# Long convolution and phase mixer: the set-up of the transform's tables rearranged

## Chip, cores and metric

The kernel runs on one core of a Trainium2 chip. The metric is the device time of one execution in microseconds, here the median of three runs. Engine names are those of the profile: PE (TensorE), PEld (its weight loads), DVE (VectorE), ACT (ScalarE), POOL (GpSimd) and SP (SyncE), which here only issues transfers.

## What is computed

```python
# x: (8, 5696, 128), h: (5696, 128)
L  = 2 * S                                   # 11392
Xf = rfft(x, n=L, axis=1); Hf = rfft(h, n=L, axis=0)
x  = irfft(Xf * Hf, n=L, axis=1)[:, :S, :]   # causal convolution, channel by channel
theta = x @ w_theta
y  = w_tok_r @ (x * cos(theta)) + w_tok_i @ (x * sin(theta))   # w_tok: 5696 x 5696
u  = x + y
out = u + relu(u @ w_ch)
```

## The kernel before

The convolution is a two-factor transform: 11392 = 178 x 64. The input is cut into 8 groups (two batches by half of the channels), and each group goes through four stages, all matmuls with DVE and ACT emptying PSUM:

- **First stage** (`stage_a`, L241): 16 chunks of four matmuls. The weights are columns of the input (`h16` or `x16`, 89 partitions by 128 columns picked with a stride), the moving operand is `f1_t`. ACT or DVE (`on_dve`) copies each chunk out.
- **Second stage** (`f2`, L260): 12 chunks, with the table `w_t2` as weights. For h, `h_chunk` (L323) scales the result into `hs` (ACT) and into `h_later` (DVE), which lies over `h16`. For x, `stage_b` (L391) copies to `xs` on ACT and multiplies with h's spectrum into `u_t` and `v_t` on DVE (L400).
- **Third stage** (`stage_c`, L410): 16 chunks with the inverse tables `r_u` and `r_v`, multiplied on the way out by the signs `sgn`, on DVE (L428) or ACT (L425, L426).
- **Fourth stage** (`stage_d`, L431): with the tables `e_t`.

h goes through the first two stages once, ahead of group 0. After that, group g's third stage is woven with group g+1's first, and its fourth with g+1's second (`woven` sorts closures by their place between 0 and 1). Then come the phases and the token mixing, which fill most of the time.

The set-up that matters here:

- h is loaded by two POOL transfers into `u_t` (L123), then copied on DVE into `h16` in two halves (L291). x's loads are 16 POOL transfers a group (`load_x`, L130) that convert to 16 bits on the way. `x16` has rows of `XP` = 68 columns, of which 64 are used; `h16` has rows of 64.
- `w_t2` has 90 slots of 192 columns. The upper and the lower 64 partitions hold the same slots shifted by 45. Sines for slots 0 to 44 are made in three blocks of 15 (`w_turns`, `w_angles`, `w_sines`). `w_rest(b)` (L203) completes a block: two scalings on DVE (L207, L208), and two copies on DVE (L210) of 64 partitions by 2880 that put each half's block into the other half's slots 45 and up. Every chunk of the second stage reads an original slot and a copied one: chunk 0 needs block 0, chunk 1 block 1 and chunk 3 block 2. `w_rest(0)` comes before h's copy, `w_rest(1)` after it, `w_rest(2)` after h's first stage.
- `h_other` (L330) and `h_store` (L335) are SP transfers: h's halves swapped within SBUF, and h stored to memory for later groups.
- `r_table(n)` (L344) makes one inverse table: index and turns on POOL (L155, L347, L351, L159), a subtraction on DVE (L162), a sine and two scalings on ACT (L168, L355, L356). `s_table` (L382) makes the signs in six small DVE instructions. Both tables and the signs are woven into group 0's second stage (L488).
- `e_index` and `e_table` make the seven steps of `e_t` likewise: POOL first, then DVE and ACT. Two steps that use the same scratch wait for one another.

Inside `in_order`, DVE, ACT and POOL keep the order of the program until L486; from there to the end of group 0's third stage DVE and ACT do, and POOL is ordered by the scheduler. `s_table` and `r_table` stood after that point, so their POOL part could be put between other POOL work:

```python
    in_order.close()
    in_order.enter_context(tc.manual_schedule(engines={mybir.EngineType.DVE, mybir.EngineType.Activation}))
    woven(b0, ([s_table, lambda: r_table(0, r_u), lambda: r_table(1, r_v)], 0.0, 0.6),
          [])
```

PSUM is used through `psum()`, four buffers of two banks, in all four stages.

Of the kernel before, what the change touches and what calls it, by code (L numbers as in the profile page):

```python
# [10 lines left out]
F32 = mybir.dt.float32  # L11
BF16 = mybir.dt.bfloat16
F16 = mybir.dt.float16
# [10 lines left out]
def kernel(  # L24
# [10 lines left out]
    nc = tc.nc  # L35
    B, S, D = x.shape
    assert D == 128
    P = 128
# [39 lines left out]
    N2 = 64  # L78
# [3 lines left out]
    KH = K1 // 2  # L82
    CK = 8
    HD = D // 2
    EN = N2 // 2 + 1
    WARM = 12
    XP = HD + 4
# [17 lines left out]
    def pool(name, bufs, stack, **kw):  # L105
        return stack.enter_context(tc.tile_pool(name=name, bufs=bufs, **kw))
# [9 lines left out]
    s1 = pool("set_1", 1, setup, side="right")  # L116
# [1 line left out]
    u_t = fc.tile([P, UVW + P], F16)  # L118
    v_t = fc.tile([P, UVW + P], F16)
    uv = [t[:, :UVW].rearrange("p (e d k) -> p e d k", e=2, k=K1) for t in (u_t, v_t)]  # L120
    h16 = s1.tile([P, 2, N2, HD], F16)
    for p0, p1 in ((0, 80), (80, NB)):
        nc.gpsimd.dma_start(u_t[p0:p1, :N2 * D],  # L123
                            bass.AP(tensor=h.tensor, offset=h.offset + p0 * N2 * D,
# [29 lines left out]
    def index(k, pattern, base):  # L154
        nc.gpsimd.iota(k, pattern=pattern, base=base, channel_multiplier=0,  # L155
                       allow_small_or_imprecise_dtypes=True)

    def up(t, k, eng=nc.vector):
        eng.tensor_scalar(k, t, MAGIC, None, op0=add)  # L159

    def below_one(t, k):
        nc.vector.scalar_tensor_tensor(t, k, MAGIC, t, op0=ALU.subtract, op1=ALU.subtract)  # L162
# [4 lines left out]
    def sine(out_, r, sign):  # L167
        nc.scalar.activation(out_, r, AF.Sin, bias=zero_b[:r.shape[0]], scale=-sign * TWO_PI)  # L168
# [4 lines left out]
    w_t2 = keep.tile([P, K1, 3 * N2], F16, tag="keep", name="w_t2")  # L173
# [3 lines left out]
    WS = 15  # L177
# [25 lines left out]
    def w_rest(b):  # L203
        s0 = WS * b
        here = w_t2[:, s0:s0 + WS]
        two = here[:, :, :2 * N2].rearrange("p k (f a n) -> p k f a n", f=2, a=2)
        nc.vector.tensor_scalar(two[:, :, :, 1], two[:, :, :, 0], odd, None, op0=mult)  # L207
        nc.vector.tensor_scalar(here[:, :, 2 * N2:], here[:, :, :N2], -1.0, None, op0=mult)  # L208
        for p0 in (0, 64):
            nc.vector.tensor_copy(w_t2[p0:p0 + 64, KH + s0:KH + s0 + WS],  # L210
                                  w_t2[64 - p0:P - p0, s0:s0 + WS])

    nc.scalar.activation(f1_t[:, :1], zero_b, AF.Sin, bias=zero_b)
    for b in range(len(w_of)):
# [22 lines left out]
    w_angles(2)  # L237
    w_sines(2)
    w_rest(0)

    def stage_a(lhs, on_dve=()):  # L241

        st = {}

        def chunk(q):
            if q == 0:
                st["a"] = fa.tile([P, 2 * K1, HD], F16, tag="a", name="a_")
            ps = psum()
            for i in range(4):
                nc.tensor.matmul(ps[:, i // 2, (i % 2) * 2 * K1:(i % 2 + 1) * 2 * K1], lhs(q + i), f1_t[:NB],  # L250
                                 start=True, stop=True)
            a_out = st["a"][:, :, q:q + 4].rearrange("p k (a q) -> p k a q", a=2)
            a_in = ps[:, :, :4 * K1].rearrange("p a (q k) -> p k a q", q=2)
            if q // 4 in on_dve:
                nc.vector.tensor_copy(a_out, a_in)
            else:
                nc.scalar.activation(a_out, a_in, AF.Copy)
        return [lambda q=q: chunk(q) for q in range(0, HD, 4)], st
# [19 lines left out]
    def woven(*lists):  # L278

        lists = [l if isinstance(l, tuple) else (l, 0.0, 1.0) for l in lists]  # L280
        steps = [(w0 + (i + 0.5) / len(l) * (w1 - w0), n, f)
                 for n, (l, w0, w1) in enumerate(lists) for i, f in enumerate(l)]
        for _, _, f in sorted(steps, key=lambda s: s[:2]):
            f()
# [7 lines left out]
                              u_t[:NB, :N2 * D].rearrange("p (n h d) -> p h n d", h=2, d=HD)[:, :, :, d0:d0 + 32])  # L292
    steps, a_h = stage_a(lambda q: h16[:NB].rearrange("p h n d -> p (h n) d")[:, :, q], (4, 6, 8, 10, 12, 14))
    w_rest(1)
    for f in steps:
        f()
    w_rest(2)

    nc.gpsimd.memset(u_t[:, UVW:], 0.0)
    nc.gpsimd.memset(v_t[:, UVW:], 0.0)  # L300
# [15 lines left out]
    def h_part(c):  # L316
        return h_flat(c).rearrange("p (r d k) -> p r d k", r=2, k=CHK[c][1])
# [5 lines left out]
    def h_chunk(c):  # L323
        c0, ck = CHK[c]
        ps = f2(a_h, c, False)
        nc.scalar.activation(h_part(c)[:, 0], ps[:, 0], AF.Copy, scale=16.0 / NF)
        nc.vector.tensor_scalar(h_later[:, HD * c0:HD * (c0 + ck)].rearrange("p (d k) -> p d k", k=ck),
                                ps[:, 1], 16.0 / NF, None, op0=mult)
# [10 lines left out]
    r_u = fc.tile([P, P], F16)  # L339
    r_v = fc.tile([P, P], F16)  # L340
    e_t = fc.tile([P, EN, 2, NB], F16)
    sgn = fc.tile([P, N2], F32)

    def r_table(n_, r_):  # L344
        t, k = (s1.tile([P, 2 * N2], F32, name=f"r_{n_}{q}") for q in "tk")
        index(k, [[0, 2], [1, N2]], 0)
        nc.gpsimd.tensor_scalar(t, k, lane[:, 0:1], 1.0 / N2, op0=mult, op1=mult)  # L347
        for q0 in range(2):
            for q1 in range(2):
                a_ = t[64 * q0:64 * q0 + 64, 64 * q1:64 * q1 + 64]  # L350
                nc.gpsimd.tensor_scalar(a_, a_, 0.25 * (1 + (1 - n_ if q0 else n_) + q0 - q1), None, op0=add)  # L351
        up(t, k, nc.gpsimd)
        below_one(t, k)
        sine(k, t, 1)
        nc.scalar.activation(r_[:, :N2 + EN], k[:, :N2 + EN], AF.Copy, scale=0.125)  # L355
        nc.scalar.activation(r_[:, N2 + EN:], k[:, N2 + EN:], AF.Copy, scale=-0.125)  # L356
# [5 lines left out]
    E_STEPS = [(n, n0, min(ES, EN - n0)) for n, n0 in enumerate(range(0, EN, ES))]  # L362
# [5 lines left out]
    def e_index(n, n0, cn):  # L368
        t, k = e_pair(n, cn)
        index(k, [[1, cn], [N2, NB]], n0)  # L370
        nc.gpsimd.tensor_scalar(t, k, lane[:K1, 1:2], 1.0 / NF, op0=mult, op1=mult)
        up(t, k, nc.gpsimd)
# [9 lines left out]
    def s_table():  # L382
        half, end = lane[:, 5:6], lane[:, 6:7]
        nc.vector.tensor_scalar(half, lane[:, 1:2], 0.0, -0.5, op0=ALU.is_equal, op1=mult)
        nc.vector.tensor_scalar(end, lane[:, 1:2], float(K1 - 1), -0.5, op0=ALU.is_equal, op1=mult)
        nc.vector.scalar_tensor_tensor(half, half, 1.0, end, op0=add, op1=add)
        nc.vector.memset(sgn, 1.0)
        nc.vector.tensor_scalar(sgn[:, :EN], sgn[:, :EN], half, None, op0=mult)
        nc.vector.tensor_scalar(sgn[:, EN:], sgn[:, EN:], odd, half, op0=mult, op1=mult)
# [76 lines left out]

    a0, b0 = front(0, (2, 4, 6, 8, 10, 12, 14))
    BATCH = ((0, 4), (4, 4), (8, 3), (11, 1))
    for c in range(NCK):
        h_chunk(c)  # L470
        for c0, n in HS:
            if c == c0 + n - 1:
                h_other(c0, n)
    for c0, n in BATCH:
        h_store(c0, n)
    for e_ in E_STEPS[:4]:
        e_index(*e_)
    for t, dst, mul in ((w_in[0], w_theta_sb, 1.0 / (2.0 * math.pi)), (w_in[1], w_ch_sb, 1.0)):
        nc.gpsimd.tensor_scalar(dst, t, mul, None, op0=mult)
    for n, f in enumerate(a0):  # L480
        f()
        if n == 9:
            e_table(*E_STEPS[0])
    load_x(1)
    e_index(*E_STEPS[4])
    in_order.close()  # L486
    in_order.enter_context(tc.manual_schedule(engines={mybir.EngineType.DVE, mybir.EngineType.Activation}))
    woven(b0, ([s_table, lambda: r_table(0, r_u), lambda: r_table(1, r_v)], 0.0, 0.6),  # L488
          [])
    e_left = [lambda f=f, n=n: f(*E_STEPS[n]) for f, n in (  # L490
        (e_table, 1), (e_index, 5), (e_table, 2), (e_index, 6), (e_table, 3),
        (e_table, 4), (e_table, 5), (e_table, 6))]
# [222 lines left out]
    for g, (bp, dh) in enumerate(groups):  # L715
        st = {}
        last = g + 1 == len(groups)
        if last:
            late_order.enter_context(tc.manual_schedule(engines={mybir.EngineType.Pool}))
        a_, b_ = front(g + 1, () if g else (5, 11))  # L720
        if last:
            for _ in range(3):
                steps0.pop(0)()
        now = [with_load(steps0.pop(0), n < 6) for n in range(9)] if last else []
        c_ = stage_c(st, last)
        if g + 2 < len(groups):
            a_ = a_ + [lambda g=g: load_x(g + 2)]
        woven((c_, 0.06 if a_ else 0.0, 1.0), (a_, 0.0, 0.55), now, ([] if g else e_left, 0.0, 0.9))
        if g == 0:
            in_order.close()  # L730
            first.close()
        if g + 2 == len(groups):
            xin.close()
            open_phases()
            load_ya0()
        now = [steps0.pop(0) for _ in range(5)] if last else []
        woven(b_, (stage_d(st, bp, dh, load_ya1 if last else None), 0.0, 1.1 if b_ else 1.0), now)
        if g + 2 == len(groups):
            load_ya1()
            open_ring()  # L740
# [320 lines left out]
    for i, (k, p, tt, j0, s0, nj) in enumerate(stretches):  # L1061
# [13 lines left out]
        if (p, tt, j0 + s0) == (0, 1, 0):  # L1075
            with tc.issue_after(sides["late"].ins):
# [4 lines left out]
        woven = (tt is not None and end_of_pair and i + 1 < len(stretches)  # L1081
                 and stretches[i + 1][2] is not None)
# [37 lines left out]
        if tt is None:  # L1120
            if p:
                aside(True, False)
            if first_of_pair:
                q = M1 if p else M3
# [16 lines left out]
            if end_of_pair:  # L1141
# [5 lines left out]
                c, c0 = c_last  # L1147
# [165 lines left out]
```

## Time and profile before

| | |
|---|---|
| median of three runs | 2041.6 us (2041.51 to 2042.7) |
| the profiled execution | 2038.09 us |
| its span | 2036.3 us |
| mean granted TensorE clock | 0.987 |
| PE busy | 1948.2 us, 96% of the span |
| DVE / POOL / ACT busy | 1574.1 / 974.3 / 654.7 us |

The span runs from the first to the last instruction of the profiled execution; 1.8 us lie around it. A row of a timeline gives the start, the busy time, the engine, the line, the operation, what it writes and reads, the count, and in brackets the idle time before it with what ended it. A row of a window gives its length, then the busy time of each engine with the count, the granted clock of PE, the share of the DMA engines (it can exceed 1, as transfers in flight are counted) and what they moved. A DMA issue is shown with its size and the time from issue to landing. Line numbers are those of the kernel before.

### The profile page before, as it was taken

What the parts mean: (1) busy time and instruction counts of PE and PEld (TensorE: products, weight loads), DVE (VectorE), ACT (ScalarE), POOL (GpSimd) and SP (SyncE); (2) the same over time, 40 slices, a digit from 0 to 9 for tenths busy, and PEclk for the clock granted to TensorE, in tenths of its full rate; (3) what the DMA queues carried; (4) which work ended last, traced back from release to release, by engine and by line L of the source; (5) the groups of instructions that cost most, each with busy time, mean ns of one, the idle gap of its engine ahead of it and who ended that gap; (6) DMA issues with size and microseconds to landing.
All of it is one profiled execution on the core that took longest, in us unless ns stands there. A gap on an engine that the chain in (4) does not pass through costs nothing.

```text
span 2036.3 us, 41470 instructions
## 1 busy us (share of the span) xinstructions
PE 1948.2 (96%) x15841; PEld 1074.5 (53%) x15841; DVE 1574.1 (77%) x2890; ACT 654.7 (32%) x1004; POOL 974.3 (48%) x1744
## 2 busy tenths in 40 slices
PE   5799999799999999999999998999999999999998
PEld 5688888654444444444444444444444444444444
DVE  8777778777788888888867668768677786777767
ACT  6788888862233323333300000111111111111111
POOL 8523321485353545454566454453544545354450
PEclk9899999899999999999999999999999999999999
DMA  9878975999798989999999799796977979788793
GB/s 117 62 84 124 88 83 167 255 268 186 161 174 179 174 171 167 181 167 181 165 176 154 117 251 220 127 154 125 154 134 138 155 128 154 129 153 140 133 156 85
DMA packets 491239, 312.56 MB, mean 153 GB/s; under 512 B 182983, under 2 KB 456007, under 8 KB 490055
## 3 DMA queue, kind: packets, MB, share of 16 engines
q0 software_dynamic: 322608, 158.13, 61.0%
q1 hardware_dynamic: 162448, 140.25, 24.1%
q10 hardware_dynamic: 5984, 11.54, 1.6%
q8 instruction: 124, 2.03, 0.4%
q14 instruction: 75, 0.61, 0.1%
HBM read 354.89 MB, written 90.82 MB: 219 GB/s over the span
## 4 chain that ended last, share of the span: by engine, by line
PE 67%; DVE 3%; DMA 3%; issue 1%; POOL 0%; ACT 0%; DVEq 0%; SPq 0%
PE m L1250 62%; DMA ring<-in_moe_w_tok_i_dram 2%; DVE c L1257 1%; PE utp L918 1%; PE v L925 1%; PE m L1254 1%; PE m L1137 1%; DVE b L776 1%; DVE wt L838 1%; PE tpz L866 0%; PE theta_ps L514 0%; POOL ring L627 0%; DMA wl<-in_moe_w_tok_i_dram 0%; DMA z_hbm<-mag 0%; DVE c L927 0%
## 5 line engine op out<-in xcount | busy, mean ns | idle before, releaser
L627 POOL DMA_DIRECT2D ring<-in_moe_w_tok_i_dram x720 | 388.2, 548 | 662.2 <-DVE wt L838 582.5
L627 POOL DMA_DIRECT2D ring<-in_moe_w_tok_r_dram x720 | 386.9, 549 | 122.6 <-DVE wt L838 64.2
L838 DVE STREAM_TRANSPOSE wt<-ring 128x384 f32<-128x384 f32 (+2 forms) x720 | 358.8, 523 | 103.2 <-PE m L1250 66.5
L1250 PE MATMUL m<-b,wt 128*128 128x512 bf16 x1640 | 388.4, 379 | 2.0 <-DVE wt L838 1.7
L1250 PEld LDWEIGHTS <-wt 128*128 128x128 bf16 x1804 | 176.0, 98 | 215.5 <-DVE wt L838 4.0
L1257 DVE TENSOR_TENSOR c<-c,m 128x512 f32<-128x512 f32 x412 | 265.3, 670 | 0.4 <-PE m L1250 0.4
L920 ACT ACTIVATE ring<-utp 128x512 bf16<-128x512 bf16 x85 | 50.8, 597 | 580.2 <-PE utp L918 580.2
L137 POOL DMA_DIRECT2D x<-in_x_dram x128 | 99.4, 798 | 141.5 <-PE ps L250 132.7
L420 PE MATMUL ps<-r_u,u_t 128*128 128x128 f16 x1024 | 125.2, 221 | 5.9 <-DVE u_t L400 2.9
L421 PE MATMUL ps<-r_v,v_t 128*128 128x128 f16 x1024 | 124.2, 220 | 0.3
L1167 PE MATMUL m<-b,wt 128*128 128x512 bf16 x480 | 112.8, 385 | 6.3 <-DMA b<-zz 2.8
L915 ACT ACTIVATE ub<-c 128x512 bf16<-128x512 f32 x88 | 55.1, 628 | 196.5 <-DMA ring<-in_moe_w_tok_i_dram 114.6
L421 PEld LDWEIGHTS <-v_t 128*128 128x128 f16 x1024 | 100.9, 99 | 5.2 <-issue 3.7
L420 PEld LDWEIGHTS <-u_t 128*128 128x128 f16 x1024 | 100.9, 99 | 3.9 <-DVE u_t L400 3.9
L398 ACT ACTIVATE xs<-ps 128x1024 f16<-128x1024 f32 x96 | 91.6, 983 | 9.6 <-PE ps L274 2.9
L400 DVE TENSOR_TENSOR u_t<-xs,hs 128x1024 f16<-128x1024 f16 x96 | 64.3, 670 | 32.1 <-ACT xs L398 29.9
L1167 PEld LDWEIGHTS <-wt 128*128 128x128 bf16 x528 | 51.1, 99 | 67.9 <-issue 4.8
L516 ACT ACTIVATE red<-theta_ps,magic 128x512 f32<-128x512 f32 (+1 forms) x46 | 31.6, 687 | 136.5 <-PE theta_ps L514 113.6
L268 PEld LDWEIGHTS <-w_t 64*128 64x128 f16 x3240 | 58.6, 100 | 23.6 <-issue 17.9
L868 ACT ACTIVATE ring<-tpz 128x512 bf16<-128x512 bf16 (+1 forms) x46 | 27.5, 597 | 130.8 <-PE tpz L866 113.7
L927 DVE SCALAR_TENSOR_TENSOR c<-v,c 128x512 f32<-128x512 f32 x88 | 59.9, 682 | 7.1 <-PE v L925 6.9
L400 DVE TENSOR_TENSOR v_t<-xs,hs 128x1024 f16<-128x1024 f16 x96 | 63.7, 664 | 0.0
(2934 smaller groups left out, 3816.1 us busy)
## 6 DMA issues: line engine op xcount, KB each, us to landing
ring<-in_moe_w_tok_r_dram POOLq DMA_DIRECT2D x352, 96.0 KB, 4.4
ring<-in_moe_w_tok_i_dram POOLq DMA_DIRECT2D x352, 96.0 KB, 4.7
ring<-in_moe_w_tok_r_dram POOLq DMA_DIRECT2D x352, 80.0 KB, 4.4
ring<-in_moe_w_tok_i_dram POOLq DMA_DIRECT2D x352, 80.0 KB, 3.9
cp_hbm<-c SPq DMA_DIRECT2D x88, 256.0 KB, 2.4
c<-cp_hbm SPq DMA_DIRECT2D x88, 256.0 KB, 4.5
out_dram<-c SPq DMA_DIRECT2D x88, 256.0 KB, 4.4
yy<-y_hbm SPq DMA_DIRECT2D x84, 128.0 KB, 2.4
```

Source lines behind the costliest of these rows:

```text
L137: nc.gpsimd.dma_start(x16[p0:p1, e, n0:n0 + 16, :HD], bass.AP(tensor=src.tensor, offset=src.offset + (p0 * N2 + n0) * D + dh * HD, ap=[[N2 ...
L268: nc.tensor.matmul(ps[:, e, j * HD:(j + 1) * HD], w_t2[rows, slot(e, c0 + j), N2 * (1 - ri):N2 * (3 - ri)], a_st["a"][rows, ri * K1 + c0 + ...
L398: nc.scalar.activation(xs[:, :, :, :ck], ps, AF.Copy)
L400: nc.vector.tensor_tensor(uv[r][:, :, :, c0:c0 + ck], xs[:, :, :, :ck], hv[:, r:r + 1].to_broadcast([P, 2, HD, ck]), op=mult)
L420: nc.tensor.matmul(o, u_t[:, at:at + P], r_u, start=True, stop=False)
L421: nc.tensor.matmul(o, v_t[:, at:at + P], r_v, start=False, stop=True)
L627: nc.gpsimd.dma_start(wb[32 * i:32 * i + 32, :ng, :nj * 64], bass.AP(tensor=a.tensor, offset=a.offset + row0 * S + p * H + i * QR + j0 * 6 ...
L838: nc.vector.transpose(wt.rearrange("p j t r -> p (j t r)").bitcast(F32).rearrange("p (j g t) -> p g j t", j=TJ, g=4)[:, :ng, :nj], wb[:, : ...
L927: nc.vector.scalar_tensor_tensor(c[:m], v[:m], 0.0, c[:m], op0=ALU.max, op1=ALU.add)
L1167: nc.tensor.matmul(ms[n // 2 * 2 + h], a[n][:, j, :, r], bts_of[p][jj][n % 2 * 2 + h][:, r, :], start=(n % 2 == 0 and jj == 0 and r == 0), ...
L1250: nc.tensor.matmul(ms[q], a[q][:, j, :, r], bts[jj][q][:, r, :], start=(jj == 0 and r == 0), stop=(jj == NJ - 1 and r == 1 and q not in left))
L1257: nc.vector.tensor_tensor(c, z, ms[q], op=op)
```

## The change

The second half of `w_t2` is filled by six SP transfers instead of six DVE copies, and `w_rest(2)` stands before h's first stage. `h16` gets rows of 68 columns. The signs and the first inverse table are made during h's second stage, the second one during group 0's first stage; their POOL part (`r_index`) stands ahead of h's second stage together with the first step of `e_index`, while three other steps of `e_index` stand after the load of group 1. Group 0's second stage is left with its own chunks alone. In group 0's third stage, group 1's first stage takes the places 0.2 to 0.75 instead of 0 to 0.55.

```diff
-    h16 = s1.tile([P, 2, N2, HD], F16)
+    h16 = s1.tile([P, 2, N2, XP], F16)
...
         for p0 in (0, 64):
-            nc.vector.tensor_copy(w_t2[p0:p0 + 64, KH + s0:KH + s0 + WS],
-                                  w_t2[64 - p0:P - p0, s0:s0 + WS])
+            nc.sync.dma_start(w_t2[p0:p0 + 64, KH + s0:KH + s0 + WS],
+                              w_t2[64 - p0:P - p0, s0:s0 + WS])
...
     w_rest(1)
+    w_rest(2)
     for f in steps:
         f()
-    w_rest(2)
...
-    def r_table(n_, r_):
-        t, k = (s1.tile([P, 2 * N2], F32, name=f"r_{n_}{q}") for q in "tk")
+    r_in = {}
+
+    def r_index(n_):
+        t, k = r_in[n_] = [s1.tile([P, 2 * N2], F32, name=f"r_{n_}{q}") for q in "tk"]
         index(k, [[0, 2], [1, N2]], 0)
...
         up(t, k, nc.gpsimd)
+
+    def r_table(n_, r_):
+        t, k = r_in[n_]
         below_one(t, k)
         sine(k, t, 1)
...
+    r_index(0)
+    r_index(1)
+    e_index(*E_STEPS[0])
     for c in range(NCK):
         h_chunk(c)
+        if c == 4:
+            s_table()
+        elif c == 9:
+            r_table(0, r_u)
...
-    for e_ in E_STEPS[:4]:
-        e_index(*e_)
+    e_index(*E_STEPS[1])
...
     for n, f in enumerate(a0):
         f()
+        if n == 2:
+            r_table(1, r_v)
         if n == 9:
             e_table(*E_STEPS[0])
     load_x(1)
-    e_index(*E_STEPS[4])
+    for e_ in E_STEPS[2:5]:
+        e_index(*e_)
...
-    woven(b0, ([s_table, lambda: r_table(0, r_u), lambda: r_table(1, r_v)], 0.0, 0.6),
-          [])
+    for f in b0:
+        f()
...
-        woven((c_, 0.06 if a_ else 0.0, 1.0), (a_, 0.0, 0.55), now, ([] if g else e_left, 0.0, 0.9))
+        woven((c_, 0.06 if a_ else 0.0, 1.0), (a_, 0.0 if g else 0.2, 0.55 if g else 0.75), now, ([] if g else e_left, 0.0, 0.9))
```

## Prediction

> **What bounds the kernel now.** I read the page first, then the windows of the set-up cut at its hand-overs, then the timeline, the tiles and the DMA issues in them. From the page:
>
> ```profile
> span 2036.3 us, 41470 instructions
> PE 1948.2 (96%) x15841; PEld 1074.5 (53%) x15841; DVE 1574.1 (77%) x2890; ACT 654.7 (32%) x1004; POOL 974.3 (48%) x1744
> ```
>
> PE is busy nearly all the time, so only an edit that lets PE begin or go on sooner can pay. The chain of waits, followed back from the end, breaks off near 530 us and does not reach the set-up. I therefore take the stages one by one. They hand over through a full wait each, and what follows (the other groups' transforms, the token mixing) is released by the stage ahead of it and not by a clock, so I carry a shift of the set-up to the end unchanged. Windows cut at PE's first instruction of each stage (columns: length, then busy time and count of PE, PEld, DVE, ACT and POOL, PE's granted clock, DMA share, GB/s):
>
> ```profile
> 0.00:16.05 16.05, 0.00 (x0) 0.01 (x1) 11.89 (x30) 7.59 (x13) 12.86 (x25) 1.00 1.75 133
> 16.05:26.75 10.70, 9.85 (x64) 9.61 (x65) 10.03 (x13) 7.38 (x10) 10.43 (x16) 1.00 1.41 85
> 26.75:35.42 8.67, 7.83 (x360) 7.44 (x360) 8.37 (x13) 6.00 (x11) 8.18 (x13) 1.00 0.34 73
> 35.42:44.30 8.88, 6.41 (x64) 5.58 (x64) 8.05 (x12) 8.01 (x13) 7.55 (x13) 1.00 0.43 95
> 44.30:66.03 21.73, 11.08 (x372) 9.94 (x371) 15.92 (x32) 13.82 (x20) 15.55 (x19) 0.66 1.32 142
> 66.03:91.95 25.92, 22.75 (x349) 22.03 (x349) 21.31 (x27) 19.96 (x33) 14.25 (x19) 0.89 0.55 35
> ```
>
> In order: tables and h's copy; h's first stage; h's second stage; group 0's first stage (x); its second stage with the products; its third stage with group 1's first. PE idles for 16 us, then is the bound in h's first stage, and is half idle in the 21.73 us of the products. DVE's timeline shows who holds the start:
>
> ```profile
> 12.40 2.06 DVE L210 COPY w_t<-w_t 64x2880 f16<-64x2880 f16 x2
> 14.49 2.68 DVE L291 COPY h<-u_t 89x4096 f16<-89x4096 f16 x2
> ...
> 27.39 2.16 DVE L210 COPY w_t<-w_t 64x2880 f16<-64x2880 f16 x2
> ...
> 29.59 4.88 DVE L327 TENSOR_SCALAR h<-ps 128x512 f16<-128x512 f32 x8
> ```
>
> h's copy begins the moment the w copies end, and PE begins at 16.05 with its first half. The third pair of w copies keeps DVE from h's second stage until 29.59. The tiles h and x, same instruction:
>
> ```profile
> L250 PEld LDWEIGHTS <-h x64: 168/174/210, 16.0 to 25.4; 89*128 89x128 f16 x64
> L250 PEld LDWEIGHTS <-x x64: 143/147/155, 35.0 to 43.1; 89*128 89x128 f16 x64
> ```
>
> Same shape, same granted clock (1.00); x has padded columns and loads faster. And in the products' stage:
>
> ```profile
> 52.48 0.40 ACT L168 ACTIVATE r_0k<-r_0t,zero_b 128x128 f32<-128x128 f32 x1 [1.56 <-DVE r_0t L162]
> ...
> 54.26 0.69 DVE L400 TENSOR_TENSOR u_t<-xs,hs 128x1024 f16<-128x1024 f16 x1 [1.81 <-ACT xs L398]
> ...
> 58.78 0.69 DVE L400 TENSOR_TENSOR u_t<-xs,hs 128x1024 f16<-128x1024 f16 x1 [1.81 <-ACT xs L398]
> ```
>
> Each inverse table makes ACT wait for DVE and then DVE for ACT.
>
> **The sum, part by part** (times from the span's start; negative is gained).
>
> *1. w copies off DVE.* DVE is free for h's copy at 12.40 instead of 14.49. h itself is later: its second transfer is issued at 2.31 and takes 10.3, so it lands at 12.6. Start 12.7 instead of 14.49: **-1.8**; PE then starts at 14.25.
>
> *2. Padded columns.* x's first stage has the same 64 matmuls and took 8.88 where h's took 10.70: **-1.8**. DVE keeps up: from 14.0 the copy's second half 1.38, w_rest(1)'s two scalings 1.24, w_rest(2)'s 1.17, six casts of 0.90, sum 9.2, ending at 23.2. That padding slows the copy itself isn't shown; its runs stay 32 columns, I take nothing. h's second stage starts at 23.15 (-3.6).
>
> *3. h's second stage* keeps its 8.67, which is PE's pace (0.72 a chunk). Added on DVE: the signs' six instructions 0.9 (47.63 to 48.5) and one subtraction 0.28, beside 7.0 of scalings (L327): 8.2. On ACT a sine and two scalings, 0.9, beside 6.4 (L326). Both stay below 8.67, so they hide in it; if that cover were gone they would cost 1.2. New is that chunks wait for the w transfers. Each of the six moves 64 x 5760 B = 360 KB. The nearest rows:
>
> ```profile
> hs<-hs SPq DMA_DIRECT2D x14, 64.0 KB, 2.7
> hs<-hs SPq DMA_DIRECT2D x2, 256.0 KB, 3.7
> hf_hbm<-h SPq DMA_DIRECT2D x1, 384.0 KB, 8.0
> ```
>
> (KB each, us from issue to landing.) So 4 to 8 us each; one issue takes SP 0.6 (L333). The first pair leaves at 12.5 and lands by 20 (due 23.2); the second leaves at 16.7, lands at 21 to 25 (due at chunk 1, 23.9); the third leaves at 18, lands at 22 to 26.6 (due at chunk 3, 25.3). A wait of 0 to 1.3: I take **+0.7**. On SP nothing is queued behind them before h's halves at 27, which the products need 15 us later.
>
> *4. POOL's queue.* r_index(0), r_index(1) and e_index(0) now stand in order behind x's load, and r_table(0) makes DVE, and ACT behind it, wait for the first. x's load shares the engines with 2.2 MB of w. The nearest row is group 1's load beside the 1.44 MB of hf stores: POOL needed 15.6 for it (43.74 to 59.34), 12.3 for the next one with nothing beside it (82.01), so 3.3 more; by bytes 4.9 here. POOL then is free of loads at 23.6 + 4.9 = 28.5. r_index is 2.9 of POOL time undisturbed (as for r_1), 4.0 disturbed (as for r_0), so it is ready at 31.4 to 32.5, against chunk 9 at 31. A wait of 0.4 to 1.5, of which the psum buffers cover some: **+0.5**. x itself landed near 25 (DMA share 0.00 from 25 to 26) and lands at 30: hidden. x's first stage starts at 33.0 instead of 35.42.
>
> *5. r_table(1) in x's first stage*: ACT 0.9, DVE 0.28, where ACT is busy 8.01 of 8.88: **+0.7**. The products start at 42.6 (was 44.30).
>
> *6. Products' stage without tables.* DVE has 11 chunks at a pitch of 1.21 and a short one of 0.7, 14.0; 2.1 before the first and 0.2 after the last: 16.3. e_index(2) to (4) now run on POOL after group 1's load, that is inside this stage; the one that did so before stretched two products by 0.35 each, so +0.7: 17.0 instead of 21.73, **-4.7**. The third stage starts at 59.6 instead of 66.03.
>
> *7. Third stage, group 1's first stage moved from 0-0.55 to 0.2-0.75.* ACT has less to do early and more late. In the second half ACT would have 6 evacuations of 0.7, 4 sign scalings of 1.15 and 4 tables of 1.15, 13.8; DVE has 12 in the first half: 25.8, as now. If the clock of PE is still at half at the start, up to 2.6 more; if the late tables overlap, or the clock is full (DVE waited 0.95 and 1.68 there on PE at half clock), up to 2.5 less. I take **+0.7**. load_x(1) starts about 2 us sooner, so x lands before its new place.
>
> Sum: -1.8 -1.8 +0.7 +0.5 +0.7 -4.7 +0.7 = **-5.7**. The profiled execution took 2038.09 (span 2036.3 and 1.8 around it), 3.5 below the median of 2041.6; its counterpart would be 2032.4, and from the median I forecast **2035.9**.
>
> [...]
>
> **Rivals.**
> *Better*: w lands in time, POOL in time, and the products without gaps keep the clock at 1.00: steps 3 and 4 give 0 and step 7 -2.0. Sum -9.6, 2032.0. For it: 310 to 368 GB/s were reached from 47 to 50. Against: the loads beside. 0.15.
> *Half rate*: 2.2 MB at 192 GB/s (the hs rows: 192 KB more take 1.0 longer), 11.5 us, all of it taken from x's load. POOL is free at 35.1, r_index(0) ready at 38, x's first stage in effect starts at 38.5. Net, with steps 5 to 7, is that start minus 38.7: -0.2, 2041.4. 0.11.
> *Padding does nothing* (h's slower loads come from something else): step 2 falls out, -3.9, 2037.7. 0.08.
> *Slower: POOL's queue becomes the bound.* Place: DVE at chunk 9, waiting for r_index(0). With d the delay of x's load and disturbed index work (4.0), the start is 23.6 + d + 4.0 + 0.5, and r_table(1) waits 2.0 more for its own index, due 1.5 later. It breaks even at d = 8.6 and is slower by 0.2% from d = 12.7; were the six transfers served with half overlap (6 x 3.7 = 22 at none), d is near 15 and the time 2048. For it: POOL did wait on x's own transfers (3.7 in all). Against: the 3.3 us beside 1.44 MB. 0.11.
>
> **How the numbers follow.** About 0.2%, 4.1 us, is what a measurement of this kernel can tell from no change. The forecast has 0.55; its centre is 1.6 beyond that bound, so I put 0.47 of it as faster and 0.08 within. Faster 0.47 + 0.15 = 0.62; within 0.08 + 0.11 + 0.08 = 0.27; slower 0.11. The range takes in the better rival and reaches up to the half rate: 2031 to 2042; left out are the slower rival and some of the two ends.
>
> **What would show it.** L250 on h at x's 147 ns and PE's first matmul near 14.3; no DVE wait ahead of the first h scaling; DVE idle ahead of r_0's subtraction below 1.5; L400 unbroken at a pitch of 0.60; the third stage starting near 59.6. Wrong if PE waits for w transfers in h's second stage for over 2 us, if x's load ends on POOL after 32, or if the third stage grows by over 3.

## The result, and the profile after

The change makes the kernel slower: 2045.54 us against 2040.73 (medians of 13 runs each), ratio 1.003 [1.0018, 1.0042]. The forecast was 2035.9 with a range of 2031 to 2042. The profiled execution took 2048.25, against 2038.09 before. Of these 10 us the set-up accounts for 5.1, close to the difference of the medians, 4.8; the rest lies in the two thousand microseconds behind it and isn't traced here (the 13 times of the kernel after alone spread from 2042.94 to 2053.06). From the page:

```profile
span 2046.5 us, 41302 instructions
PE 1940.1 (95%) x15664; PEld 1075.9 (53%) x15841; DVE 1568.9 (77%) x2884; ACT 654.3 (32%) x1004; POOL 970.1 (47%) x1744
```

The windows, cut at the same hand-overs as before (length, then busy time and count of PE, PEld, DVE, ACT and POOL, PE's granted clock, DMA share, GB/s):

```profile
0.00:14.03 14.03, 0.00 (x0) 0.00 (x1) 9.54 (x28) 7.59 (x13) 10.84 (x23) 1.00 1.51 132
14.03:24.71 10.68, 9.82 (x65) 9.59 (x65) 8.85 (x11) 7.38 (x10) 6.91 (x9) 1.00 1.90 152
24.71:41.24 16.53, 10.00 (x360) 9.26 (x360) 7.12 (x16) 5.86 (x10) 8.73 (x21) 0.92 1.50 170
41.24:53.35 12.11, 9.99 (x68) 9.54 (x65) 8.73 (x14) 9.63 (x19) 4.51 (x7) 0.50 0.51 164
53.35:69.72 16.37, 8.67 (x361) 8.12 (x360) 14.03 (x24) 11.48 (x12) 12.22 (x17) 0.71 1.46 92
69.72:98.14 28.42, 22.96 (x361) 21.89 (x362) 22.20 (x27) 21.04 (x35) 18.52 (x24) 0.95 0.33 22
```

Against before the lengths went by -2.0 (start), 0.0 (h's first stage), +7.9 (h's second), +3.2 (x's first), -5.4 (products), +2.5 (third stage): +6.2 where group 1's second stage begins, and +5.1 at its third stage. One border isn't the same in both kernels: before, 12 matmuls of group 1's first stage ran ahead of 66.03 (372 matmuls in the products' row and 349 in the next), and after, none did (361 and 361). Some work thus moved from the products to the third stage, and -5.4 and +2.5 are best read together, as -2.9.

PE's timeline of the long third row, in the kernel before:

```profile
26.75 6.59 PE L268 MATMUL ps<-a__184,w_t 64*128 64x64 f16 x287 [0.86 <-ACT a__184 L257]
33.83 1.24 PE L268 MATMUL ps<-a__184,w_t 64*128 64x64 f16 x73 [0.48 <-issue]
35.42 5.92 PE L250 MATMUL ps<-f_t,x 89*128 89x180 f16 x56 [0.36 <-DVE h L327]
```

And in the kernel after:

```profile
24.71 1.81 PE L268 MATMUL ps<-a__188,w_t 64*128 64x64 f16 x61 [0.86 <-ACT a__188 L257]
28.23 1.90 PE L268 MATMUL ps<-a__188,w_t 64*128 64x64 f16 x62 [1.71 <-DMA w_t<-w_t]
30.78 0.24 PE L268 MATMUL ps<-a__188,w_t 64*128 64x64 f16 x2 [0.64 <-DVE h L327]
31.53 1.14 PE L268 MATMUL ps<-a__188,w_t 64*128 64x64 f16 x34 [0.52 <-DMA w_t<-w_t]
33.26 2.86 PE L268 MATMUL ps<-a__188,w_t 64*128 64x64 f16 x128 [0.59 <-issue]
39.18 2.13 PE L268 MATMUL ps<-a__188,w_t 64*128 64x64 f16 x73 [3.06 <-issue]
```

The idle times, 1.71 + 0.64 + 0.52 + 0.59 + 3.06 = 6.5, and 10.0 of work (7.83 before) make the 16.5. PE waits twice for copies of w that are still in flight, and for 3.06 us for nothing that the profile names. The transfers of x in the kernel before (KB each, median us from issue to landing) and POOL's first issue behind x's load:

```profile
x<-in_x_dram POOLq DMA_DIRECT2D x8, 160.0 KB, 5.5
```

```profile
22.15 0.59 POOL L289 DMA_DIRECT2D w_in<-in_moe_w_theta_dram  x1
```

The same in the kernel after, with the transfers of w:

```profile
w_t<-w_t SPq DMA_DIRECT2D x6, 360.0 KB, 10.8
x<-in_x_dram POOLq DMA_DIRECT2D x8, 160.0 KB, 12.8
```

```profile
31.53 0.59 POOL L289 DMA_DIRECT2D w_in<-in_moe_w_theta_dram  x1 [7.25 <-DMA x<-in_x_dram]
```

I had taken 4 to 8 us for a w transfer: they took 7.8 to 12.6. Six of them leave from 12.42 to 19.63, and the last lands at 31.5. x's load, which runs beside them, suffers as much: its 160 KB pieces needed 5.5 us before and 12.8 now (those issued after 14 us: 4.1 to 4.9 before, 16.9 to 17.8 now), and POOL came to the issue behind them 9.4 us later. And the tile x, first before and then after:

```profile
L250 PE MATMUL ps<-f_t,x x64: 237/241/241, 35.4 to 43.2; 89*128 89x180 f16 x64
```

```profile
L250 PEld LDWEIGHTS <-x x64: 147/168/173, 41.2 to 52.0; 89*128 89x128 f16 x64
L250 PE MATMUL ps<-f_t,x x64: 310/356/373, 41.2 to 52.1; 89*128 89x180 f16 x64
```

After the gaps PE's granted clock is 0.50, and x with its padded columns shows the very figures that h showed without padding.

### The profile page after: what moved, and what is told of

Same layout as the page of the kernel before. It is cut to its first block, busy times and chain, and to the rows that moved or that the text cites. A ratio compares the mean times of both kernels' runs of the same rounds, so it can differ in the third digit from the quotient of the medians.

```text
span 2046.5 us, 41302 instructions
## 1 busy us (share of the span) xinstructions
PE 1940.1 (95%) x15664; PEld 1075.9 (53%) x15841; DVE 1568.9 (77%) x2884; ACT 654.3 (32%) x1004; POOL 970.1 (47%) x1744
## 4 chain that ended last, share of the span: by engine, by line
PE 67%; DMA 3%; DVE 2%; issue 1%; POOL 0%; ACT 0%; DVEq 0%; SPq 0%
PE m L1264 62%; DMA b<-z_hbm 1%; DVE c L1271 1%; PE utp L932 1%; PE v L939 1%; PE m L1268 1%; PE m L1151 1%; PE theta_ps L528 0%; PE tpz L880 0%; DVE wt L852 0%; POOL ring L641 0%; DMA cp_hbm<-c 0%; DMA c<-cp_hbm 0%; DVE b L790 0%; PE m L1181 0%
## 5 line engine op out<-in xcount | busy, mean ns | idle before, releaser
L1264 PE MATMUL m<-b,wt 128*128 128x512 bf16 x1598 | 384.4, 379 | 4.2 <-DVE wt L852 1.7
L1181 PE MATMUL m<-b,wt 128*128 128x512 bf16 x465 | 110.5, 383 | 11.3 <-DMA b<-z_hbm 7.7
```

What stands on the lines that cost most here:

```text
L1181: nc.tensor.matmul(ms[n // 2 * 2 + h], a[n][:, j, :, r], bts_of[p][jj][n % 2 * 2 + h][:, r, :], start=(n % 2 == 0 and jj == 0 and r == 0), ...
L1264: nc.tensor.matmul(ms[q], a[q][:, j, :, r], bts[jj][q][:, r, :], start=(jj == 0 and r == 0), stop=(jj == NJ - 1 and r == 1 and q not in left))
```

## The experiments

Starts of the stages in one profiled execution each (us). "Products" is group 0's second stage; "fourth" is the start of group 1's second stage (the first `xs` on ACT), "third of g1" that of group 1's third stage (its first sign product on DVE), the last point compared. The last column is the median minus that of the kernel before on the same chip, where several rounds were run.

| kernel | h 1st | h 2nd | x 1st | products | fourth | third of g1 | median |
|---|---|---|---|---|---|---|---|
| before | 16.05 | 26.75 | 35.42 | 44.30 | 91.95 | 111.21 | |
| after | 14.03 | 24.71 | 41.24 | 53.35 | 98.14 | 116.31 | +4.8 |
| pad_only | 16.06 | 26.74 | 36.24 | 45.11 | 92.64 | 110.79 | |
| warm_only | 15.85 | 27.13 | 36.40 | 45.56 | 92.64 | 110.78 | -1.2 |
| w_only | 14.40 | 25.10 | 40.49 | 51.25 | 98.22 | 116.37 | +3.5 |
| w_alone | 14.32 | 25.00 | 41.05 | 53.15 | 98.37 | 116.77 | |
| w_alone2 | 14.00 | 24.68 | 47.50 | 58.16 | 104.39 | 122.59 | |
| tables_only | 16.04 | 26.75 | 36.01 | 48.30 | 93.52 | 112.20 | +1.4 |
| tables_keepwarm | 16.02 | 26.73 | 38.07 | 48.13 | 93.15 | 111.67 | |
| tables_weave | 16.25 | 26.95 | 36.21 | 48.10 | 92.83 | 110.97 | |
| split | 16.08 | 26.78 | 36.07 | 45.43 | 92.49 | 110.93 | -0.9 |
| before_store | 16.16 | 26.87 | 35.43 | 44.33 | 91.94 | 110.23 | -0.5 |
| split_store | 16.16 | 26.86 | 36.15 | 45.52 | 88.23 | 106.44 | -3.1 |
| split_store_late | 16.04 | 26.75 | 36.03 | 45.68 | 94.08 | 112.23 | +1.0 |

The shift of group 1's third stage and the change of the median go together within 1.7 us in all eight timed kernels (after +5.1 and +4.8, split_store -4.8 and -3.1). That a shift of the set-up is carried to the end was thus a fair reading.

**pad_only: the padded columns alone.**

```diff
-    h16 = s1.tile([P, 2, N2, HD], F16)
+    h16 = s1.tile([P, 2, N2, XP], F16)
```

> The kernel before with h's rows padded to 68 columns, nothing else. Theory A (clock): h's loads stay at 174 ns and the first stage at 10.7. Theory C (stride): 147 ns and about 8.9.

The tile h in the kernel before, and both its rows in this kernel:

```profile
L250 PE MATMUL ps<-f_t,h x64: 334/356/393, 16.1 to 25.5; 89*128 89x180 f16 x64
```

```profile
L250 PEld LDWEIGHTS <-h x64: 147/168/171, 16.1 to 25.4; 89*128 89x128 f16 x64
L250 PE MATMUL ps<-f_t,h x64: 318/356/375, 16.1 to 25.5; 89*128 89x180 f16 x64
```

Padding takes 6 ns off a weight load (174 to 168) and nothing off the stage, which lasts 10.68 instead of 10.70 (2037.74 in one run). My cause for the difference between h and x was wrong. 356 ns is what x's matmuls take in the kernel after, at a granted clock of 0.50.

**warm_only: 130 throw-away matmuls ahead of h's first stage**, on the kernel before, into columns of the first chunk's PSUM buffer that the chunk leaves unused.

```diff
             ps = psum()
+            if q == 0:
+                for n in range(warm):   # 130 for h, 0 for x
+                    nc.tensor.matmul(ps[:, n % 2, 384:512], ident_bf, ident_bf, start=True, stop=True)
```

> The kernel before with 130 throw-away matmuls of 128 columns on PE ahead of h's first stage, in the time in which PE waits for h; h's columns stay unpadded. Theory A (h's weight loads are slow because PE still runs at half clock, whatever the record of the clock says): h's matmuls and loads go from 356 and 174 ns to x's 241 and 147, the stage from 10.7 to about 9, and the time falls by 1 to 3 (2038 to 2040). Theory C (the column stride makes them slow): 356 and 174 stay, and the time with them.

2038.81 against 2039.97, ratio 0.9996 [0.9984, 1.0008]. Windows of it (the clock is the third figure from the right):

```profile
16.00:20.00 4.00, 4.00 (x29) 4.00 (x30) 3.92 (x5) 3.26 (x5) 4.00 (x5) 0.54 1.25 77
20.00:24.00 4.00, 3.35 (x24) 3.17 (x23) 3.97 (x5) 1.91 (x4) 4.00 (x9) 0.50 1.60 100
```

The extra work ended at 11.6, PE then idled until 15.85, and h's matmuls stayed at 356 ns (PE busy 0.15 of the 4 us from 12 to 16). But here the record itself reads 0.54 and 0.50, where the same durations stood under 1.00 before. So h's first stage runs at half clock, and the 1.00 of the kernel before, ahead of the first change of the clock in its records, says nothing. "Same granted clock", on which my step 2 stood, was read off this 1.00. What full clock would be worth in h's first stage stays open, as the warm-up did not last; that DVE is busy 3.9 of 4.0 us there argues for little, but no run shows it.

**w_only: the w transfers and the earlier `w_rest(2)` alone.**

```diff
-            nc.vector.tensor_copy(w_t2[p0:p0 + 64, KH + s0:KH + s0 + WS],
-                                  w_t2[64 - p0:P - p0, s0:s0 + WS])
+            nc.sync.dma_start(w_t2[p0:p0 + 64, KH + s0:KH + s0 + WS],
+                              w_t2[64 - p0:P - p0, s0:s0 + WS])
...
     w_rest(1)
+    w_rest(2)
     for f in steps:
         f()
-    w_rest(2)
```

> The kernel before, with only the w halves moved to SP transfers and w_rest(2) ahead of h's first stage (nothing else of the change). Theory A (the w transfers are what costs: 2.2 MB taken out of x's load, so that they land late, x lands late, and PE falls to half clock): h's first stage starts near 14.0 but h's second stage has waits on w, x's first stage starts after 39 instead of 35.42 and takes over 11; 2045 to 2051. Theory B (the loss comes from the index tables behind x's load on POOL, not from the transfers): x's first stage starts near 33, and the time is 2037 to 2040.

2043.45 against 2039.97, ratio 1.0018 [1.0005, 1.003]. PE's timeline:

```profile
28.69 1.90 PE L268 MATMUL ps<-a__188,w_t 64*128 64x64 f16 x62 [1.78 <-DMA w_t<-w_t]
32.22 1.14 PE L268 MATMUL ps<-a__188,w_t 64*128 64x64 f16 x34 [0.75 <-DMA w_t<-w_t]
```

The same two waits, with no table moved and no index in the way. h's second stage takes 15.4, x's first 10.76 instead of 8.88 (matmuls 358 ns), and group 1's third stage is 5.16 late. This edit alone gives the whole shift of the set-up (5.16 against 5.10 in the whole change) and 3.5 of the 4.8 us between the medians; the two intervals overlap.

**w_alone, w_alone2: the same transfers with nothing beside them.** The first puts `load_x(0)` behind `w_rest(2)`, to be issued after the last w transfer's issue.

```diff
-    load_x(0)
...
     w_rest(1)
     w_rest(2)
+    with tc.issue_after(w_last[0].ins):   # the last w transfer
+        load_x(0)
```

> The changed kernel with x's first load issued only after the last w transfer, so that the w transfers run with nothing beside them (the time of the kernel is not the point: x comes late by design). If sharing with x's load is what makes them 8 to 12.6 us each: 3.5 to 5 each, w's two waits in h's second stage gone. [...]

2046.84 in one run, and inconclusive: x's load wasn't held back. Its first four pieces were issued from 6.30 and the others from 12.06, and w took 10.2 beside them. The second puts the load at the same place and makes it wait for the landings: POOL first reads one element of each copied part into the x buffer.

```diff
-    load_x(0)
...
     w_rest(2)
+    load_x(0)
...
+        if g == 0:                        # in load_x, ahead of its transfers
+            for n_ in (0, 64):
+                for s_ in (KH, KH + WS, KH + 2 * WS):
+                    nc.gpsimd.tensor_copy(x16[n_:n_ + 1, 0, 0, s_ - KH:s_ - KH + 1], w_t2[n_:n_ + 1, s_, 0:1])
```

> The changed kernel with x's first load held back, by six one-element copies on POOL that read what the w transfers write, until all six have landed: now the w transfers really run with only h's load ahead of them (the time is not the point, x comes late by design). If x's load beside them is what makes them 8 to 13 each: 3.5 to 5.5 each, and no wait on w in h's second stage. If they are slow in themselves: the later pairs stay at 6 or more, and x's load, which then runs alone, needs its 17.

The issues between 12 and 25 us:

```profile
w_t<-w_t SPq DMA_DIRECT2D x6, 360.0 KB, 4.8
```

And PE's timeline of h's second stage:

```profile
24.68 3.51 PE L272 MATMUL ps<-a__194,w_t 64*128 64x64 f16 x123 [0.86 <-ACT a__194 L261]
...
34.79 1.24 PE L272 MATMUL ps<-a__194,w_t 64*128 64x64 f16 x73 [1.66 <-issue]
```

Alone, a transfer lands in 3.6 to 6.3 us (the first two pairs in 4.2, the last in 6.1), in the main inside my 4 to 8, and PE never waits for w. So the size I took was that of an undisturbed transfer. As a version it is useless (2049.85 in one run): x lands too late, and x's first stage starts at 47.50. Here the rival "POOL's queue" does appear at its place: DVE waits 6.72 at chunk 9 for r_0's index, which stands behind the late load.

The 2.21 MB moved between 13.0 and 23.4, that is in 10.4 us. The 11.5 us that the rival "half rate" took for them is thus near for the transfers alone. The rate behind it isn't borne out: in the unbroken stretch from 19.0 to 23.4 the trace has 251 GB/s, above its 192. The 251 are for one stream, and the loss lies in two: side by side both loads are slowed, w from a median of 4.8 to 10.8 and x's from 5.5 to 12.8. In what order their packets are served the trace doesn't show.

**tables_only: the change without the transfers and the padding.** DVE copies w, `w_rest(2)` is back behind h's steps, `h16` has 64 columns; signs, tables, indexes and the new places of group 1's first stage are as changed.

> The changed kernel with the w copies back on DVE, w_rest(2) back behind h's first stage, and unpadded h: only the moved tables, signs, index work and group 1's first stage are left of the change. Theory A: the set-up keeps its 44.3 to within 1 until the products, these take 16.4 to 17 instead of 21.7 (third stage starts near 61.5), and the third stage gives back 0 to 2.5; 2036 to 2039. Theory B: DVE waits for r_0's index at chunk 9 of h's second stage, the products start after 46, and the time is 2041 or more.

2041.36 against 2039.97, ratio 1.0004 [0.9993, 1.0016]. The products' stage drops from 21.73 to 16.4, as forecast, and the gain is lost on both sides of it. Ahead of it the timelines of DVE, ACT and PE show:

```profile
36.47 0.28 DVE L162 SCALAR_TENSOR_TENSOR r_0t<-r_0k,r_0t 128x128 f32<-128x128 f32 x1
36.79 0.40 ACT L168 ACTIVATE r_0k<-r_0t,zero_b 128x128 f32<-128x128 f32 x1 [1.07 <-DVE r_0t L162]
...
38.14 0.89 DVE L327 TENSOR_SCALAR h<-ps 128x512 f16<-128x512 f32 x2 [1.39 <-ACT hs L326]
38.88 8.56 PE L250 MATMUL ps<-f_t,x 89*128 89x180 f16 x56 [1.80 <-DVE h L327]
```

The table stands at chunk 9 in both engines' orders. ACT waits 1.07 for DVE's subtraction, then makes the table while the last chunks stand in PSUM; DVE waits 1.39 for ACT's part of them, and PE, which needs their buffers for x, waits 1.80. POOL's index was not the cause: it was ready by 27. So theory A has the products right, theory B the start behind 46 and the time, but not the cause. In x's stage the 8 matmuls ahead of this wait take 240 ns, and those behind it 356 to 359; the recorded clock falls from 1.00 to 0.50 near 38. The stage takes 12.3.

**tables_keepwarm: tables_only with throw-away matmuls in h's second stage**, to hold the clock.

```diff
-        ps = f2(a_h, c, False)
+        ps = f2(a_h, c, True)
```

> Moved tables only, as in tables_only, plus 12 throw-away matmuls of 384 columns behind the last chunk of h's second stage, which fill PE's wait ahead of group 0's first stage. Theory D (the wait of 1.8 us that the first inverse table makes there also drops PE to half clock, and that is most of what the stage lost): the matmuls of group 0's first stage are back at 241 ns instead of 356, the stage takes at most 10.5 instead of 12.3, and the products start near 46.5 instead of 48.30. Rival E (the ping-pong of DVE and ACT alone is the price): 356 ns or not, the stage stays above 11.8.

2040.02 in one run. The tile x:

```profile
L250 PE MATMUL ps<-f_t,x x64: 238/241/359, 38.1 to 46.9; 89*128 89x180 f16 x64
```

PE's longest wait between them is 0.55 us, where tables_only has 1.80. Most matmuls are back at 241 ns, so that wait is what took the clock down, and the stage takes 10.06, as theory D has it. Yet the products start at 48.13 instead of 48.30: the extra work holds PE for some 2 us itself (36.11 to 38.07). So this run cannot price the clock, and it leaves the interleaving of the table as the candidate.

**tables_weave: tables_only with group 1's first stage back at 0 to 0.55.**

```diff
-        woven(..., (a_, 0.0 if g else 0.2, 0.55 if g else 0.75), ...)
+        woven(..., (a_, 0.0, 0.55), ...)
```

> Moved tables only, as in tables_only, but with group 1's first stage at 0 to 0.55 of the third stage as before. Theory F (its later place is what makes the third stage 28.7 instead of 25.9): 25.5 to 26.5. Rival (group 1's x lands too late for the old place, or DVE's tables hold it): 28 or more, with PE waiting for x in its first microseconds.

2038.35 in one run. PE's timeline at the start of the third stage:

```profile
65.48 2.00 PE L250 MATMUL ps<-f_t,x 89*128 89x180 f16 x12 [5.92 <-DMA x<-in_x_dram]
```

Now the third stage waits for group 1's x. Its load begins at 47.54, when group 0's first stage has ended (there is one `x16` buffer), and lands 18 us after it begins. This is the rival's case. An earlier third stage has no x to work on: the fourth starts at 92.83 instead of 93.52. The later places hid that wait and paid for it with a longer stage.

**split: no table inside a chain.** On tables_only: the subtractions go to chunks 1 and 3 of x's first stage, the sines to 6 and 8, and the places become 0.1 to 0.65.

```diff
-        elif c == 9:
-            r_table(0, r_u)
...
-        if n == 2:
-            r_table(1, r_v)
+        if n in (1, 3):
+            r_turn(n // 2)                          # the subtraction on DVE
+        elif n in (6, 8):
+            r_table(n // 2 - 3, (r_u, r_v)[n // 2 - 3])   # the sine and two scalings on ACT
```

> Moved tables only, but the inverse tables are made in group 0's first stage in two steps: the subtractions on DVE after chunks 1 and 3, the sines on ACT after chunks 6 and 8, so that neither engine waits for the other; group 1's first stage at 0.1 to 0.65. Theory D: group 0's first stage starts near 35.8, keeps full clock and takes 9 to 10; products start near 45.5, the third stage near 62; ratio to the kernel before 0.998 to 0.9990 (3 us less in the median). Rival E: the added work itself takes the stage to 11 or more, and the time is that of before within 0.1%.

2040.44 against 2041.3, ratio 1.0 [0.999, 1.001]. x's first stage takes 9.36 with both tables in it, at full clock (241 ns); so of the 3.4 us by which this stage had grown in tables_only, 2.9 were the ping-pong and the half clock behind it, which this run doesn't tell apart. The stage is as theory D has it, and the time as rival E has it. The third stage now starts 3.5 earlier than before (62.58), and the fourth starts at 92.49 all the same: the gain goes into the third stage.

**before_store, split_store, split_store_late: h's stores earlier.** Each `h_store` is issued in the loop as soon as its chunks are done, so that fewer of them run beside the load of group 1's x; on the kernel before, on split with the places 0 to 0.55, and on split with 0.1 to 0.65.

```diff
                 h_other(c0, n)
-    for c0, n in BATCH:
-        h_store(c0, n)
+        for c0, n in BATCH:
+            if c == c0 + n - 1:
+                h_store(c0, n)
```

> The kernel before, with the four stores of h's spectrum issued between the swaps of its halves instead of after them (they then run before group 1's load, not beside it). Theory H (the third stage's end is set by group 1's x, which lands some 18 us after group 0's first stage ends, because the stores share its time): POOL needs 12.5 instead of 15.6 for group 1's load, x lands 3 earlier, and the third stage ends 1 to 3 earlier (fourth stage from 89 to 91 instead of 91.95). Rival I (the third stage is bound by the work of ACT and DVE): the load is faster, but the end stays at 91.5 to 92.5.

2039.76 against 2040.25, ratio 0.9997 [0.9985, 1.0008]. x's load is quicker (POOL needs 13.9 for it instead of 15.6), but the fourth stage starts at 91.94, as before: in the kernel before, the arrival of x doesn't set the end of the third stage. That the work of DVE and ACT does, as rival I has it, is what is left; this run doesn't show it by itself.

> As split (tables in two steps in group 0's first stage, DVE copies for w), with the early stores, and group 1's first stage at 0 to 0.55. Theory H: x lands near 60.5, the third stage starts near 62 and ends at 87 to 89.5; 2035 to 2038, ratio near 0.998. Rival I: the end stays at 92 to 93 and the time at that of before.

2037.11 against 2040.25, ratio 0.9984 [0.9974, 0.9993]: 3.1 us better than the kernel before, and better than the kernel after. The gain is below the 0.2% that I named as the limit of one measurement, but its interval lies wholly below 1. PE's timeline at the start of the third stage:

```profile
61.83 2.00 PE L250 MATMUL ps<-f_t,x 89*128 89x180 f16 x12 [5.27 <-DMA x<-in_x_dram]
```

x lands 3.7 us earlier than in tables_weave, 2.6 of it because the load starts earlier; the rest I put down to less being in its way. Three things came together: the products without tables, x's load with two stores beside it instead of four, and group 1's first stage at the front of the third. The run that leaves out the early stores alone is missing; tables_weave, with the tables elsewhere, is the nearest.

> The same with group 1's first stage at 0.1 to 0.65. Theory H: like split_store within 1 us, since x has landed by then in either. Rival I: 92 to 93.

2041.21, ratio 1.001 [1.0001, 1.0018]. The places alone cost 5.9 us at the fourth stage (94.08), which neither theory had. The waits from 62 to 94 us (in total, times, longest):

```profile
DVE g__1321 L435 <- PE ps L428: 9.3, 7, 2.6
ACT a__1340 L257 <- PE ps L250: 6.7, 5, 3.2
```

With x in time, a late place makes DVE and ACT wait for PE by turns.

## Why the prediction was wrong

- *Step 1, DVE free for h's copy*: right. PE started at 14.03, forecast 14.25.
- *Step 2, padding*: wrong in its cause; 0.0 instead of -1.8. I took two tiles at "clock 1.00" as compared at the same clock. The matmuls themselves differed too, 356 ns for h against 241 for x, in the same view of the tiles; padding touches only what the weight loads read, and this should have stopped me. The rival "padding does nothing" had this part right, at 0.08.
- *Step 3, the wait for w, and step 4, x's load displaced*: the terms that failed. +0.7 and +0.5 were forecast, and h's second stage took 7.9 more. The two waits for w, 2.2 us together, are over the 2 us that the prediction named as a sign of being wrong. I sized w's transfers by rows without another load beside them, though I had x's load displaced by w in the very next step: the same contention had to stand in both. w_alone2 shows the undisturbed size (4.8), w_only the disturbed one (11.3) and its price. Of the 7.9, the two waits for w are 2.2, the named idle times on DVE and the short issue 1.2, the unnamed gap 2.6 more than before, and PE's own work 2.2 more, as more of it runs at half clock (below); 0.4 goes off for a wait on DVE that stood at the end before. The unnamed gap can't be booked to the w transfers: it is 1.44 in w_only, where the stage takes 6.7 more, and 1.96 in tables_keepwarm, which has no such transfers.
- The displacement of x's load was 9.4 us on POOL and some 13 at landing (38.3 against 25.0) instead of 4.9. The rival "POOL's queue becomes the bound" had it right that d is over 8.6 and the kernel slower. Its place was wrong for this kernel. DVE didn't stop at chunk 9 for `r_index(0)`; its subtraction came at 41.52, more than five microseconds after the index was ready (36.0). PE had stopped earlier, for w, and even x had landed by the time that h's second stage was through. So its 2048, the nearest of the times that I gave, came near by luck: with the 9.4 of POOL as d its sum gives +0.8, and the 15 that I put in doesn't follow from the 22 of six transfers either, half of which is 11.
- *Step 5, the second table in x's first stage*: +3.2 instead of +0.7. Of this 1.9 is the half clock that follows the gaps (w_only, with no table there: 10.76) and 1.3 the table at chunk 9 (PE's wait of 1.26 for DVE in the kernel after). That is the first table; behind that wait PE runs x's other 56 matmuls without a gap (8.56 us), so the second one, which the +0.7 stood for, shows no wait of PE. The step that failed is step 3's "they hide in it". I had asked only whether the table's work hides in h's second stage (8.2 of 8.67) and not how it stands in order between ACT and DVE, though I had read that very pattern off the products' stage.
- *Step 6, the products' stage*: right in kind and near in size, -5.4 against -4.7, of which some is group 1's matmuls that moved behind the border. The clock of the old stage fell from 1.00 to 0.50 between 54 and 56, that is behind the first of PE's three long waits there (2.81 us) and ahead of the other two (2.56 and 2.69).
- *Step 7, the third stage*: +2.5 instead of +0.7. I added up the work of DVE and ACT (25.8) and took that as the length, but with the later places they also wait for PE: DVE 5.2 us in the kernel after (3.3 before), and split_store_late prices such places at 5.9. The early start that I forecast would have bought little by itself: the transfers of group 1's x go on to near 60 us in before_store, 62 in the kernel before and 68 in the kernel after.

What stays open is the length of the unnamed gap. It stands behind the same 287 matmuls of h's second stage in nearly every kernel: 0.48 before, 0.36 in before_store, 1.18 in tables_only, 1.96 in tables_keepwarm, and with the w transfers 1.44 in w_only, 1.66 in w_alone2 and 3.06 after. Its place in PE's order is nearly the same in all of them. In the kernel after, the short gap of 0.59 stands 128 matmuls ahead of it. The next one comes 382 matmuls behind it, nearly three times as many, before, after and in tables_keepwarm, where 12 of them are the extra ones. The 130 matmuls that warm_only puts ahead of everything move the place only by 2, to 285. The trace has transfers of the kind "instruction" near several of these gaps: two in the kernel before between 30 and 33, one in tables_only between 32 and 34.5, two in the kernel after between 35.5 and 39.3. What PE waits for there these runs don't show, nor whether the gap would shrink if w came earlier.

## What to carry to other kernels

Before a copy is moved from an engine to a transfer, list what else is in flight in the same microseconds and size both streams together: here the six landed in a median of 4.8 us alone and of 10.8 beside x's load. A small table placed in two engines' orders cost the ping-pong between them here (in tables_only ACT waited 1.07, DVE 1.39 and PE 1.80), not its busy time, so its parts go to places where the other engine's part has long been done. The shorter products' stage paid here once the load of the next stage's input was freed of stores too (-0.9 us in split, -3.1 in split_store); find the load behind a stage first.

## What was unexpected of the hardware

In the kernel before the windows read a granted clock of 1.00 until the first change is recorded, also where the matmuls take 356 ns, so here the clock of the start had to be read off the durations. By them PE runs at half clock from its first matmul at 16.05 until near 30. In the kernel before, the matmuls of h's second stage, from 26 to 30 and from 30 to 33 us (count, then min/median/max in ns; at a recorded 0.50, from 45 to 46.8, the same shape takes 238, and at a recorded 1.00, from 48 to 50, 190):

```profile
L268 PE MATMUL ps<-a__184,w_t x123: 207/238/238, 26.8 to 30.0; 64*128 64x64 f16 x123
L268 PE MATMUL ps<-a__184,w_t x161: 186/190/238, 29.8 to 33.0; 64*128 64x64 f16 x161
```

The change from 238 to 190 comes near 30 us, 14 us after PE began, with an idle time of 0.86 in between and 9.85 of the first 10.70 busy. No single length of work goes with it: counted from 26.75, the end of that idle time, the change comes after 3.3 to 3.8 us, while h's first stage ahead of it and, in the kernel after, x's behind the gaps (12.11 us at a recorded 0.50, of which 8.56 without a gap) bring none. What raises the clock these runs don't show. In the kernel after, the durations come down to 190 only near 35 us, and behind the gap of 3.06 the last 73 matmuls of the stage have a median of 238 again. A wait in the set-up thus cost more than its own length; this is where I put the 2.2 us of additional work and the 1.9 us in x's first stage.
